# Row maxima of an attention kernel: one negated row at partition 0 by a Prelu, in place of two rows by a Relu

## The chip, the cores and the metric

The kernel runs on one core of a Trainium2 chip. Its metric is the device time of one execution in microseconds (us), and lower is better. Four compute engines work side by side, each in its own program order: PE (TensorE, matmuls), DVE (VectorE), ACT (ScalarE) and POOL (GpSimd). SP issues all DMAs. PEld is PE's loading of the stationary operand, which the profile keeps apart from the matmuls themselves.

## The reference

Attention over pooled queries, then a channel-mixing feed-forward. The sizes are 8 batches, 8 heads, 1152 keys, 576 pooled queries and a head size of 64; the model width is 512 and the hidden width 1024.

```python
q_pool = q.reshape(B, H, S // 2, 2, D).mean(axis=3)
scores = (1 / sqrt(D)) * (q_pool @ k.T)
scores = scores - max(scores, axis=-1, keepdims=True)
attn = exp(scores)
attn = attn / (sum(attn, axis=-1, keepdims=True) + 1e-9)
x = attn @ v                                   # heads side by side: (B, 576, 512)

x_prev = x shifted by one position, zeros in front
xk = mu_k * x + (1 - mu_k) * x_prev            # xr the same with mu_r
kk = maximum(xk @ w_k, 0)
out = sigmoid(xr @ w_r) * (kk * kk @ w_v)
```

## The kernel before, in words

**Precision.** Products are made of fp16 parts. A value is split into a high part and a low part, and the products high x high, high x low and low x high are added in PSUM.

**A block** (`block`, L527) is one head's 96 queries against all its 1152 keys. There are 64 heads of 6 blocks, 384 blocks in all. The keys lie in nine chunks of 128. A block owns one of three PSUM buffers `s`: columns 0 to 127 are scratch, and the nine 128x96 score tiles lie behind them. Its steps, in the order in which they depend on each other:

- L549, PE: nine matmuls, the first half of the scores. The stationary operand is a key chunk `ks1` (high parts of the key in partitions 0 to 63, low parts in 64 to 127), the moving operand is `qT` with the high parts of the queries.
- L556, DVE: the maximum over the nine chunks, `mx` (128x96).
- L559, PE: `mx` as stationary operand against the identity gives the transposed maxima in the scratch columns, 96 partitions by 128.
- L563, DVE: the maximum along the 128 columns, `mb` (96x1): each query's own maximum.
- L579, PE: `mb`, spread over 128 columns, against a scaled negative identity turns the maxima back into a row, which then stands in every partition of the scratch.
- L583, ACT: this row goes into the operand of the second half of the scores, `qlo` (the part of `qT` with the low parts of the queries in partitions 0 to 63). A Relu with a scale per partition (the tile `sign`, +1 and -1) writes two rows, 96 and 97: one holds what is positive and one what is negative of it.
- L592, PE: nine matmuls, the second half: `ks2` against `qlo`. `ks2` has the high key parts in partitions 0 to 63 (a DMA at L505 copies them from `ks1`) and two constant rows at 96 and 97 (`lift`, L405 and L411), which take the maximum off every score within the same matmul.
- L598, ACT: the exponential of the nine tiles into `pf`. L606, POOL: its low part `pl`.

**Around it.** `queries` (L420) and `prep` (L481) load and split a head's inputs. After the first heads a DMA transposes them (L460, L503). `window` (L642) multiplies probabilities with values (L656, L658, L663 on PE), divides (L679 to L682 on DVE), and after each second head turns the result by PE transposes (L692) and copies it out of the PSUM bank `a` into `xt` with four copies (L702, ACT): two of 64x64, two of 128x256. `halves` (L627) does the same for the two ends of a head that do not fill a tile. `ff` makes the feed-forward of a finished batch (all matmuls at L842) while the next batch's attention runs; the last batch's feed-forward runs alone at the end. `weights` decodes the weights early in the program (DMAs at L720; L732, L734 and L749 on ACT, L744 and L747 on DVE).

**What sets the order.** Every piece of work is recorded with `op(engine, cost, function, reads, writes, key)`. The class `Issue` then plays a list schedule with these costs, improves it forwards and backwards, and shifts the priorities of random groups of operations by the numbers in `MOVES`. Each engine issues its instructions in the order that comes out. So the cost that is written beside an operation takes part in the order, and `MOVES`, `BASE`, `SEED`, `SPREAD` and `HALF` choose it.

Of the kernel before, what the change touches and what calls it, by code (L numbers as in the profile page):

```python
# [37 lines left out]
EPS = 2.0 ** -9  # L38
ROW, ROW_N = "AA", 0
# [16 lines left out]
HALF = 1.1  # L56
# [11 lines left out]
SEED, SPREAD = 2, 5.0  # L68
# [227 lines left out]
def kernel(  # L296
# [37 lines left out]
    def bufs(name, n, shape, dt):  # L334
        return [const.tile(shape, dt, name=f"{name}{i}") for i in range(n)]
# [34 lines left out]
    mx, mb, mt = bufs("mx", 3, [P, QN], F16), bufs("mb", 3, [P, 1], F16), bufs("mt", 3, [P, 1], F32)  # L370
# [31 lines left out]
    nc.gpsimd.memset(qn[0][:, 1, :, D:P], 0.0)  # L402
    sign, lift = const.tile([P, 1], F32, name="sign"), const.tile([P, 1], F32, name="lift")
    for c_, a_, b_ in ((sign, -2.0, 1.0), (lift, -2.0 * SM, SM * (1.0 - EPS))):
        nc.vector.tensor_scalar(c_, ident[:, QN + 1:QN + 2], a_, b_, op0=ALU.mult, op1=ALU.add)  # L405
    negd = const.tile([P, P], F16, name="negd")
    nc.gpsimd.tensor_scalar(negd, ident, EPS - 1.0, 1.0, op0=ALU.mult, op1=ALU.mult)
    for t_ in ks2:
        nc.vector.memset(t_[D:P], 0.0)
        nc.vector.memset(t_[QN:QN + 2], 1.0)  # L410
        nc.vector.tensor_scalar(t_[QN:QN + 2], t_[QN:QN + 2], lift[QN:QN + 2], None, op0=ALU.mult)  # L411
# [8 lines left out]
    def queries(n, key):  # L420
# [16 lines left out]
        for j0, j1 in JS:  # L437
            js, jk = slice(j0, j1), range(j0, j1)
            for nj, ck, o_, src in pieces(j0, j1):
# [10 lines left out]
                qn[0][:, 1, js, 0:D], qs[0][:, js], SQ, qn[0][:, 0, js, 0:D], op0=ALU.mult, op1=ALU.subtract),  # L450
# [30 lines left out]
    def prep(n, key):  # L481
# [23 lines left out]
        op("DMA", 0.54, lambda: nc.sync.dma_start(ks2[i][0:D], ks1[i][0:D]),  # L505
# [21 lines left out]
    def block(n, j, i, t):  # L527
# [10 lines left out]
        mxz, mbz, mtz = mx[z], mb[z], mt[z]  # L538
        row = ROW[int(n >= ROW_N)]
# [12 lines left out]
        for c0, c1 in BK:  # L552
# [3 lines left out]
        op("DVE", 0.975, lambda: nc.vector.tensor_reduce(mxz, grid(0, NC).rearrange("p c q -> p q c"),  # L556
                                                         axis=AX.X, op=ALU.max),
           r=[("s", z)], w=[("mx", z)], key=t)
        op("PE", 0.059, lambda: nc.tensor.matmul(s[0:QN, 0:P], mxz, identb, start=False, stop=False,  # L559
                                                 skip_group_check=True),  # L560
           r=[("mx", z)], w=[("s", z)], key=t + O_MAX)
        if row == "A":
            op("DVE", 0.199, lambda: nc.vector.tensor_reduce(mbz[0:QN], s[0:QN, 0:P], axis=AX.X, op=ALU.max),  # L563
               r=[("s", z)], w=[("mb", z)], key=t + O_MAX)
        else:
            op("DVE", 0.199, lambda: nc.vector.tensor_reduce(mtz[0:QN], s[0:QN, 0:P], axis=AX.X, op=ALU.max),
               r=[("s", z)], w=[("mt", z)], key=t + O_MAX)
            op("DVE", 0.07, lambda: nc.vector.tensor_scalar(
                mbz[0:QN], mtz[0:QN], 1.0 + 2.0 * EPS, mtz[0:QN], op0=ALU.mult, op1=ALU.max),
               r=[("mt", z)], w=[("mb", z)], key=t + O_MAX)  # L570
        if row == "D":
            def lower(c0, c1):
                for c in range(c0, c1):
                    nc.tensor.matmul(cols(c, c + 1), mbz[0:QN].broadcast_to([QN, P]), negd[0:QN, 0:QN],
                                     start=False, stop=False, skip_group_check=True)

            op("PE", NC * 0.0430, lambda: lower(0, NC), r=[("mb", z)], w=[("s", z)], key=t + O_MAX)
        else:
            op("PE", 0.047, lambda: nc.tensor.matmul(s[:, 0:QN], mbz[0:QN].broadcast_to([QN, P]),  # L579
                                                     negi[0:QN, 0:QN], start=False, stop=False, skip_group_check=True),  # L580
               r=[("mb", z)], w=[("s", z)], key=t + O_MAX)
            if row == "A":
                op("ACT", 0.267, lambda: nc.scalar.activation(qlo[QN:QN + 2], s[QN:QN + 2, 0:QN], AF.Relu,  # L583
                                                              scale=sign[QN:QN + 2]),
                   r=[("s", z)] + kl, w=qm, key=t + O_MAX)
            else:
                op("ACT", 0.175, lambda: nc.scalar.copy(qlo[QN:QN + 1], s[QN:QN + 1, 0:QN]),
                   r=[("s", z)] + kl, w=qm, key=t + O_MAX)
# [6 lines left out]
        for c0, c1 in BK:  # L595
            op("PE", (c1 - c0) * 0.0430, lambda c0=c0, c1=c1: scores2(c0, c1),
               r=[("ks2", hp)] + kl + (qm if row != "D" else []), w=[("s", z)], key=t + O_EXP)
# [390 lines left out]
```

## Time and profile before

| | |
|---|---|
| Median of 3 runs | 1172.43 us (1170.05 to 1173.1) |
| Profiled execution | 1174.95 us, of which the span from the first to the last instruction is 1173.2 us |
| Busy in the span | PE 1116.6, ACT 947.3, DVE 900.7, POOL 527.5 us |
| TensorE clock granted | 0.987 of full speed over the span, 0.89 between 15 and 150 us |

A row such as `L583 ACT ACTIVATE qT<-s,sign 2x96 f16<-2x96 f32 x384 | 124.7, 332 | 71.5 <-PE s L579 56.9` reads: the line, the engine, the operation, what it writes and reads with shapes, how often; then its busy time in us, the mean duration of one in ns, and the idle time of its engine just before it with what ended most of that. Matmuls overlap: a row's mean is the time from a matmul's start to its result, far more than the distance between two starts. So PE's idle time in these rows is only what is longer than that overlap. The chain of waits is followed back from the last instruction, at each step to what released it.

### The profile page before, as it was taken

Reading aid. Unit: us, or ns where it says so; the run is one execution under the profiler, and the core shown is the slowest. Engines: PE = TensorE matmul, PEld = TensorE weight load, DVE = VectorE, ACT = ScalarE, POOL = GpSimd, SP = SyncE. Lnnn points to the kernel's source line nnn. Section 1 sums busy time; section 2 is a strip of 40 time slices with the busy share of each in tenths; the row PEclk is TensorE's granted clock in tenths of the full one; section 3 lists DMA queues with packets and bytes.
Section 4 is the critical chain, followed back from the end, with each engine's and each line's share of the span. In section 5 each row is a group of like instructions: output and inputs, shape, how many; then the busy total and the mean of one; then the engine's idle time right before and its main releaser. Section 6 shows DMA issues by size and latency. Waiting matters only on the chain.

```text
span 1173.2 us, 44732 instructions
## 1 busy us (share of the span) xinstructions
PE 1116.6 (95%) x18956; PEld 912.8 (78%) x18956; DVE 900.7 (77%) x1849; ACT 947.3 (81%) x1947; POOL 527.5 (45%) x574
## 2 busy tenths in 40 slices
PE   5887799999999999999999999999999999999998
PEld 4776787978788787878787888868797878888665
DVE  8888888888788888887888788777888788774531
ACT  7899988978888888888978887877878788876753
POOL 2456554644445444544443554435354444443111
PEclk9888899999999999999999999999999999999999
DMA  9986756555455643755354435344453734310000
GB/s 204 204 177 159 184 116 126 118 108 131 99 132 112 113 117 81 133 110 136 83 125 94 120 91 129 94 95 103 112 119 70 140 84 92 60 38 10 21 19 27
DMA packets 218744, 125.71 MB, mean 107 GB/s; under 512 B 154032, under 2 KB 190896, under 8 KB 218544
## 3 DMA queue, kind: packets, MB, share of 16 engines
q1 hardware_dynamic: 218544, 122.86, 47.7%
q8 instruction: 148, 2.42, 0.9%
q14 instruction: 52, 0.43, 0.1%
HBM read 67.11 MB, written 9.44 MB: 65 GB/s over the span
## 4 chain that ended last, share of the span: by engine, by line
PE 73%; ACT 12%; DMA 6%; DVE 5%; issue 4%; SPq 0%; ACTq 0%; DVEq 0%
PE f L842 27%; PE s L549 11%; PE s L592 10%; PE a L658 5%; PE a L656 5%; PE a L663 5%; ACT pf L598 4%; PE s L842 4%; DMA ks<-kn 4%; DVE mx L556 2%; ACT qT L583 2%; PE a L627 2%; PE s L559 2%; PE a L842 2%; PE s L579 1%
## 5 line engine op out<-in xcount | busy, mean ns | idle before, releaser
L606 POOL TENSOR_SCALAR pl<-pf 128x864 f16<-128x864 uint16 x384 | 370.4, 965 | 452.3 <-ACT pf L598 419.6
L556 DVE TENSOR_REDUCE mx<-s 128x96 f16<-128x864 f32 x384 | 398.9, 1053 | 97.3 <-PE s L549 59.8
L598 ACT ACTIVATE pf<-s 128x864 int32<-128x864 f32 x384 | 334.9, 889 | 45.3 <-PE s L592 29.4
L549 PE MATMUL s<-qT,ks 128*128 128x96 f16 x3456 | 222.4, 208 | 22.6 <-ACT pf L598 18.0
L549 PEld LDWEIGHTS <-ks 128*128 128x128 f16 x3456 | 188.8, 99 | 58.0 <-issue 32.2
L592 PE MATMUL s<-qT,ks 128*128 128x96 f16 x3456 | 214.4, 208 | 12.4 <-ACT qT L583 10.7
L592 PEld LDWEIGHTS <-ks 128*128 128x128 f16 x3456 | 182.4, 99 | 38.7 <-issue 19.0
L656 PE MATMUL a<-vt,pf 128*128 128x65 f16 x2304 | 196.0, 194 | 1.0 <-DVE a L640 0.6
L658 PE MATMUL a<-vt,pf 128*128 128x64 f16 x2304 | 196.3, 195 | 0.0
L583 ACT ACTIVATE qT<-s,sign 2x96 f16<-2x96 f32 x384 | 124.7, 332 | 71.5 <-PE s L579 56.9
L656 PEld LDWEIGHTS <-pf 128*128 128x128 f16 x2304 | 164.9, 99 | 5.2 <-ACT pf L598 0.5
L658 PEld LDWEIGHTS <-pf 128*128 128x128 f16 x2304 | 157.4, 98 | 7.6 <-issue 1.5
L563 DVE TENSOR_REDUCE mb<-s 96x1 f16<-96x128 f32 x384 | 107.5, 283 | 46.5 <-PE s L559 41.5
L842 PE MATMUL f<-xhk,wk_hi 128*128 128x256 f16 x496 | 135.1, 272 | 1.1 <-ACT r L869 0.7
L842 PE MATMUL f<-xlk,wk_hi 128*128 128x256 f16 x496 | 135.1, 272 | 0.0
L842 PE MATMUL f<-xhk,wk_lo 128*128 128x256 f16 x496 | 135.1, 272 | 0.0
L873 POOL TENSOR_TENSOR gl<-g 128x512 f16<-128x512 f32 x72 | 78.6, 1093 | 107.3 <-ACT g L871 104.4
L663 PE MATMUL a<-vb,pl 128*128 128x65 f16 x2304 | 122.8, 194 | 0.1
L842 PEld LDWEIGHTS <-wk_hi 128*128 128x128 f16 x1152 | 107.0, 98 | 12.9 <-issue 1.3
L663 PEld LDWEIGHTS <-pl 128*128 128x128 f16 x2304 | 97.6, 98 | 4.4 <-POOL pl L606 0.3
L559 PE MATMUL s<-identb,mx 128*96 128x128 f16 x384 | 87.1, 228 | 5.6 <-DVE mx L556 5.3
L842 PE MATMUL f<-wv_hi,g 128*128 128x512 f16 x240 | 90.9, 379 | 0.7 <-ACT em L892 0.6
(113 smaller groups left out, 2046.4 us busy)
## 6 DMA issues: line engine op xcount, KB each, us to landing
kr<-in_k_dram SPq DMA_DIRECT2D x64, 288.0 KB
vr<-in_v_dram SPq DMA_DIRECT2D x64, 288.0 KB
qr<-in_q_dram SPq DMA_DIRECT2D x63, 256.0 KB
ks<-ks SPq DMA_DIRECT2D x64, 144.0 KB
out_dram<-em SPq DMA_DIRECT2D x36, 256.0 KB
st<-in_moe_w_k_dram SPq DMA_DIRECT2D x8, 512.0 KB
st<-in_moe_w_v_dram SPq DMA_DIRECT2D x8, 512.0 KB
qr<-in_q_dram SPq DMA_DIRECT2D x32, 64.0 KB
```

What stands on the lines that cost most here:

```text
L549: nc.tensor.matmul(cols(c, c + 1), ks1[hp][:, c, :], qhi, start=(c == c0), stop=False, skip_group_check=True)
L556: op("DVE", 0.975, lambda: nc.vector.tensor_reduce(mxz, grid(0, NC).rearrange("p c q -> p q c"), axis=AX.X, op=ALU.max), r=[("s", z)], w=[ ...
L559: op("PE", 0.059, lambda: nc.tensor.matmul(s[0:QN, 0:P], mxz, identb, start=False, stop=False, skip_group_check=True), r=[("mx", z)], w=[( ...
L563: op("DVE", 0.199, lambda: nc.vector.tensor_reduce(mbz[0:QN], s[0:QN, 0:P], axis=AX.X, op=ALU.max), r=[("s", z)], w=[("mb", z)], key=t + O ...
L583: op("ACT", 0.267, lambda: nc.scalar.activation(qlo[QN:QN + 2], s[QN:QN + 2, 0:QN], AF.Relu, scale=sign[QN:QN + 2]), r=[("s", z)] + kl, w= ...
L592: nc.tensor.matmul(cols(c, c + 1), ks2[hp][:, c, :], qlo, start=False, stop=True, skip_group_check=True)
L598: op("ACT", NC * QN / 1200 + 0.06, lambda: nc.scalar.activation(pf[:, :, rows], grid(0, NC), AF.Exp, bias=SHIFT, scale=0.125 / (2.0 * SQ)) ...
L606: op(pe, d, lambda: en.tensor_scalar(pl[:, :, rows], half(pf, U16, 0)[:, :, rows], LO, 1.0, op0=ALU.mult, op1=ALU.mult), r=[("pf", x) for ...
L656: nc.tensor.matmul(bank[:, a0:a0 + VN], half(pf, F16, 1)[:, c, rows], vt[jv][:, c, D:D + VN], start=(w == 1 and c == 0 and hh == 0), stop= ...
L658: nc.tensor.matmul(bank[:, a0:a0 + D], half(pf, F16, 1)[:, c, rows], vt[jv][:, c, 0:D], start=False, stop=False, skip_group_check=True)
L663: nc.tensor.matmul(bank[:, a0:a0 + VN], pl[:, c, rows], vb[jv][:, c, 0:VN], start=False, stop=(c == NC - 1), skip_group_check=True)
L842: nc.tensor.matmul(ps, terms[i][0], terms[i][1], start=(first and i == 0), stop=(i == last), skip_group_check=True)
```

## The change

1. **One row by a Prelu.** L583's Relu with the scale tile `sign` becomes a Prelu with two constants, a scale and an `alpha` for negative inputs. It writes one row, of 1x96, at partition 0. The constant row of `ks2` (L407 after) stands at partition 0 too and is written by a single memset. The tiles `sign`, `lift`, `negd` and `mt`, and the variants of the row that did not run, go.
2. **Low query parts in partitions 64 to 127.** `qlo` and the high key parts in `ks2` move from partitions 0 to 63 up to 64 to 127; the DMA that fills `ks2` now goes from partitions 0 to 63 to partitions 64 to 127.
3. **Transposed maxima with 32 zero columns in front.** `mx` becomes 128x128, with its first 32 columns zeroed once. The stationary operand of the transposing matmul has 128 columns where it had 96, its output 128 partitions, `mb` is 128x1, and the matmul that turns it back works over 128 partitions.
4. **Copies.** Of the four copies out of bank `a` after the transposes, the 64x64 one of partitions 64 to 127 moves from ACT to DVE.
5. **Order.** The costs of the row (0.267 to 0.153) and of `halves` (1.1 to 1.02) change, and the numbers that choose the order are new. `EPS`, by which the row's two slopes differ from 1, is 2**-10 where it was 2**-9.

```diff
-EPS = 2.0 ** -9
-ROW, ROW_N = "AA", 0
+EPS = 2.0 ** -10
+ROW = "Prelu"
...
-HALF = 1.1
+HALF = 1.02
...
-    12, 57, 71, 78, 82, 116, 127, 165, 204, 389, 459, 497, 555, 573, 765, 911, 920, 1257, 1370, 1565, 1944,
...
-), 3000000, 1150.0
-SEED, SPREAD = 2, 5.0
+    35, 45, 48, 64, 96, 102, 107, 118, 189, 197, 445, 511, 603, 622, 676, 682, 702, 806, 807, 882, 1095, 1109,
...
+), 4000000, 1150.0
+SEED, SPREAD = 2, 3.0
...
-    mx, mb, mt = bufs("mx", 3, [P, QN], F16), bufs("mb", 3, [P, 1], F16), bufs("mt", 3, [P, 1], F32)
+    mx, mb = bufs("mx", 3, [P, P], F16), bufs("mb", 3, [P, 1], F16)
...
-    nc.gpsimd.memset(qn[0][:, 1, :, D:P], 0.0)
-    sign, lift = const.tile([P, 1], F32, name="sign"), const.tile([P, 1], F32, name="lift")
-    for c_, a_, b_ in ((sign, -2.0, 1.0), (lift, -2.0 * SM, SM * (1.0 - EPS))):
-        nc.vector.tensor_scalar(c_, ident[:, QN + 1:QN + 2], a_, b_, op0=ALU.mult, op1=ALU.add)
-    negd = const.tile([P, P], F16, name="negd")
-    nc.gpsimd.tensor_scalar(negd, ident, EPS - 1.0, 1.0, op0=ALU.mult, op1=ALU.mult)
+    nc.gpsimd.memset(qn[0][:, 1, :, 0:D], 0.0)
+    for t_ in mx:
+        nc.vector.memset(t_[:, 0:P - QN], 0.0)
     for t_ in ks2:
-        nc.vector.memset(t_[D:P], 0.0)
-        nc.vector.memset(t_[QN:QN + 2], 1.0)
-        nc.vector.tensor_scalar(t_[QN:QN + 2], t_[QN:QN + 2], lift[QN:QN + 2], None, op0=ALU.mult)
+        nc.vector.memset(t_[0:D], 0.0)
+        nc.vector.memset(t_[0:1], SM)
...
-        op("DMA", 0.54, lambda: nc.sync.dma_start(ks2[i][0:D], ks1[i][0:D]),
+        op("DMA", 0.54, lambda: nc.sync.dma_start(ks2[i][D:P], ks1[i][0:D]),
...
-        op("DVE", 0.975, lambda: nc.vector.tensor_reduce(mxz, grid(0, NC).rearrange("p c q -> p q c"),
+        op("DVE", 0.975, lambda: nc.vector.tensor_reduce(mxz[:, P - QN:P], grid(0, NC).rearrange("p c q -> p q c"),
                                                          axis=AX.X, op=ALU.max),
...
-        op("PE", 0.059, lambda: nc.tensor.matmul(s[0:QN, 0:P], mxz, identb, start=False, stop=False,
-                                                 skip_group_check=True),
+        op("PE", 0.059, lambda: nc.tensor.matmul(s[:, 0:P], mxz, identb, start=False, stop=False, skip_group_check=True),
...
+        op("DVE", 0.199, lambda: nc.vector.tensor_reduce(mbz, s[:, 0:P], axis=AX.X, op=ALU.max),
+           r=[("s", z)], w=[("mb", z)], key=t + O_MAX)
+        op("PE", 0.047, lambda: nc.tensor.matmul(s[:, 0:QN], mbz.broadcast_to([P, P]), negi[:, P - QN:P],
+                                                 start=False, stop=False, skip_group_check=True),
+           r=[("mb", z)], w=[("s", z)], key=t + O_MAX)
+        op("ACT", 0.153, lambda: nc.scalar.activation(qlo[0:1], s[0:1, 0:QN], getattr(AF, ROW),
+                                                      scale=1.0 - EPS, alpha=(1.0 + EPS) / (1.0 - EPS)),
+           r=[("s", z)] + kl, w=qm, key=t + O_MAX)
...
-                op("ACT", 0.051 + (q1 - q0) / 1200, lambda ps=ps, q0=q0, q1=q1, f0=f0, x_=x_: nc.scalar.copy(
+                up = y == 1
+                op("DVE" if up else "ACT", 0.07 + HW / 960 if up else 0.051 + (q1 - q0) / 1200, lambda up=up, ps=ps, q0=q0, q1=q1, f0=f0, x_=x_: (nc.vector.tensor_copy if up else nc.scalar.copy)(
                     x_[ps, 1 + q0:1 + q1], bank[ps, f0:f0 + q1 - q0]),
                    r=[ka], w=[("xt", b % 3, g, y)], key=t + O_TURN)
```

How the order moves is shown at three places. In the rows a number behind a name tells buffers apart.

The first is DVE at the start of the program, from the first head's low key parts to the first maximum. Before:

```order
L496 TENSOR_TENSOR kn_76<-kr_70,kn_76 128x4x64
L513 SCALAR_TENSOR_TENSOR vt_85<-vr_72,vt_85 128x4x64
L442 TENSOR_TENSOR qs_75<-qr_74 128x128
L405 TENSOR_SCALAR sign<-ident 128x1
L405 TENSOR_SCALAR lift<-ident 128x1
L411 TENSOR_SCALAR ks_0_81<-ks_0_81,lift 2x1152
L411 TENSOR_SCALAR ks_1_82<-ks_1_82,lift 2x1152
L478 COPY ks_0_79<-s_138 128x512
```

After the change, the same place:

```order
L492 TENSOR_TENSOR kn_76<-kr_70,kn_76 128x5x64
L438 TENSOR_TENSOR qs_75<-qr_74 128x128
L438 TENSOR_TENSOR qs_75<-qr_74 128x192
L445 SCALAR_TENSOR_TENSOR qn_78<-qs_75,qn_78 128x2x64
L404 MEMSET mx_93 128x16
L474 COPY ks_0_79<-s_135 128x512
```

The four instructions on `sign`, `lift` and `ks2` between the first key parts and the copy of the transposed keys are gone. The value split `vt` moves behind; the second query sum, the first low query parts and one memset of `mx` move ahead of the copy.

The second is ACT in the stage in which the weights are decoded, around the first copies into `xt`. Before:

```order
L517 ACTIVATE vb_89<-vr_72 128x9x64
L583 ACTIVATE qT_84<-s_136,sign 2x96
L702 COPY xt_106<-a 128x256
L702 COPY xt_106<-a 64x64 x2
L810 ACTIVATE tmp_123<-xt_106,omu_k 128x256
L598 ACTIVATE pf<-s_136 128x9x96
L732 ACTIVATE f<-st_129 128x512
L583 ACTIVATE qT_84<-s_138,sign 2x96
```

After the change:

```order
L678 COPY xt_103<-a 128x256
L678 COPY xt_103<-a 64x64
L561 ACTIVATE qT_84<-s_133 1x96
L708 ACTIVATE f<-st_126 128x512
L678 COPY xt_103<-a 128x256
L710 ACTIVATE em_124<-st_126 128x512
L573 ACTIVATE pf<-s_133 128x9x96
L513 ACTIVATE vb_89<-vr_72 128x9x64
L786 ACTIVATE tmp_120<-xt_103,omu_k 128x256
```

The two 64x64 copies of a turn have become one on ACT, and the row (L583, after it L561) reads no scale tile. The copies and the decoding have moved ahead of the splitting of the values `vb`.

The third is DVE at the same turn, where the copy that left ACT now stands (L678). Before:

```order
L679 TENSOR_SCALAR den_103<-a 128x5
L556 TENSOR_REDUCE mx_93<-s_136 128x96
L681 RECIPROCAL den_103<-den_103 128x5
L682 TENSOR_TENSOR xb_104<-a,den_103 128x5x64
L563 TENSOR_REDUCE mb_96<-s_136 96x1
L513 SCALAR_TENSOR_TENSOR vt_85<-vr_73,vt_85 128x5x64
L556 TENSOR_REDUCE mx_95<-s_138 128x96
```

After the change:

```order
L657 TENSOR_TENSOR xb_101<-a,den_100 128x5x64
L551 TENSOR_REDUCE mx_93<-s_133 128x96
L445 SCALAR_TENSOR_TENSOR qn_78<-qs_75,qn_78 128x4x64
L556 TENSOR_REDUCE mb_96<-s_133 128x1
L678 COPY xt_103<-a 64x64
L551 TENSOR_REDUCE mx_94<-s_134 128x96
L551 TENSOR_REDUCE mx_95<-s_135 128x96
```

The copy stands between the maximum of one block and the two long maxima of the next two blocks, which wait behind it in DVE's queue.

More of the change, by code (lines that the diff above doesn't have):

```diff
@@ L449, in queries @@
             op("DVE", (j1 - j0) * D / 960 + 0.069, lambda js=js: nc.vector.scalar_tensor_tensor(
-                qn[0][:, 1, js, 0:D], qs[0][:, js], SQ, qn[0][:, 0, js, 0:D], op0=ALU.mult, op1=ALU.subtract),
+                qn[0][:, 1, js, D:P], qs[0][:, js], SQ, qn[0][:, 0, js, 0:D], op0=ALU.mult, op1=ALU.subtract),
                r=[("qs", c) for c in jk] + [("qn", c) for c in jk], w=[("qnl", c) for c in jk], key=key + 2, port=True)
@@ L537, in block @@
         rows, us = slice(p0, p0 + QN), range(p0 // U, (p0 + QN) // U)
-        mxz, mbz, mtz = mx[z], mb[z], mt[z]
-        row = ROW[int(n >= ROW_N)]
+        mxz, mbz = mx[z], mb[z]
         def cols(c0, c1):
@@ L561, in block @@
            r=[("mx", z)], w=[("s", z)], key=t + O_MAX)
[L562 to L588, printed above, removed]
+        op("DVE", 0.199, lambda: nc.vector.tensor_reduce(mbz, s[:, 0:P], axis=AX.X, op=ALU.max),
+           r=[("s", z)], w=[("mb", z)], key=t + O_MAX)
@@ L596, in block @@
             op("PE", (c1 - c0) * 0.0430, lambda c0=c0, c1=c1: scores2(c0, c1),
-               r=[("ks2", hp)] + kl + (qm if row != "D" else []), w=[("s", z)], key=t + O_EXP)
+               r=[("ks2", hp)] + kl + qm, w=[("s", z)], key=t + O_EXP)
         op("ACT", NC * QN / 1200 + 0.06, lambda: nc.scalar.activation(
```

10 rows, old and new, of the table AHEAD2 are left out of this document.

## The prediction, made before the changed kernel ran

> **What bounds the kernel now.** I read the busy table first.
>
> ```profile
> span 1173.2 us, 44732 instructions
> PE 1116.6 (95%) x18956; PEld 912.8 (78%) x18956; DVE 900.7 (77%) x1849; ACT 947.3 (81%) x1947; POOL 527.5 (45%) x574
> ```
>
> PE is idle for 1173.2 - 1116.6 = 56.6 us, so anything that only takes work off ACT or DVE must pay through these 56.6 us or through idle time too short to show behind the overlap of matmuls. The view by stages tells where they lie (columns: time, then busy us and instructions of each engine, granted clock, DMA share):
>
> ```profile
> core 0: us, PE busy (x) PEld busy (x) DVE busy (x) ACT busy (x) POOL busy (x), PEclk, DMA share, GB/s
> 0.00:15.00 15.00, 6.44 (x68) 5.28 (x69) 12.21 (x37) 9.92 (x22) 2.11 (x10) 1.00 0.74 209
> 15.00:150.00 135.00, 106.37 (x2121) 95.21 (x2121) 115.50 (x232) 125.24 (x242) 74.28 (x77) 0.89 0.83 181
> 150.00:1075.00 925.00, 909.39 (x16119) 754.20 (x16117) 740.78 (x1518) 763.87 (x1581) 437.25 (x474) 1.00 0.48 104
> 1075.00:1173.20 98.20, 94.45 (x652) 58.06 (x650) 32.22 (x64) 48.28 (x104) 13.86 (x14) 1.00 0.06 22
> ```
>
> PE's idle time is 8.6 us in the start, 28.6 in the stage with the weight decoding (15 to 150 us), 15.6 in the long middle and 3.7 in the last feed-forward, where no block runs. In the second stage ACT is the fullest engine, 125.2 of 135 us, and in its core it hardly pauses:
>
> ```profile
> 60.00:90.00 30.00, 24.73 (x504) 21.78 (x501) 26.26 (x50) 29.19 (x55) 17.42 (x19) 0.89 0.93 177
> 90.00:120.00 30.00, 23.03 (x456) 20.62 (x453) 24.09 (x48) 29.31 (x58) 19.30 (x20) 0.89 0.64 167
> ```
>
> 58.5 of 60 us: that stage is ACT's. In the middle PE itself is the bound. PE's longest waits (who waited for whom, us in total, times, longest), between 15 and 150 us:
>
> ```profile
> PE s L549 <- ACT pf L598: 12.6, 24, 1.1
> PE s L592 <- ACT qT L583: 6.7, 15, 0.9
> ```
>
> and between 150 and 1075 us:
>
> ```profile
> PE s L549 <- ACT pf L598: 5.4, 12, 1.4
> PE s L592 <- ACT qT L583: 4.0, 6, 1.4
> ```
>
> The chain of waits by line, for the start and the two attention stages:
>
> ```profile
> by line: DVE ks L410 13.6%; issue 12.8%; PE s L549 10.7%; DVE ks L409 7.2%; ACT vt L510 7.0%; DVE ks L411 6.4%; ACT qT L475 5.1%; ACT ks L475 4.8%; ACT vb L517 3.8%; ACT qn L445 3.5%; DVE kn L496 3.2%; ACT kn L493 3.1%; DVE ks L478 2.9%; AC
> ...
> by line: ACT pf L598 13.7%; issue 11.4%; PE s L549 10.4%; DVE mx L556 7.7%; PE s L592 6.5%; ACT qT L583 5.4%; ACT f L732 5.0%; ACT em L734 4.9%; PE a L656 3.8%; PE a L658 3.6%; DMA ks<-ks 3.6%; PE a L663 2.8%; ACT vt L510 2.5%; DMA ks<-kn 2
> ...
> by line: PE f L842 32.2%; PE s L549 12.1%; PE s L592 11.3%; PE a L663 5.3%; PE a L658 5.2%; PE a L656 5.2%; DMA ks<-kn 4.8%; ACT pf L598 3.5%; issue 2.8%; PE a L627 2.2%; PE s L559 1.8%; DVE mx L556 1.6%; ACT qT L583 1.6%; PE s L579 1.3%; P
> ```
>
> So L583, the instruction that changes, is on the chain for 5.4% of 135 = 7.3 us in the second stage and 1.6% of 925 = 14.8 us in the middle.
>
> **The change part by part.** The groups that carry the prices:
>
> ```profile
> L583 ACT ACTIVATE qT<-s,sign 2x96 f16<-2x96 f32 x384 | 124.7, 332 | 71.5 <-PE s L579 56.9 <-DVE mb L563 2.9 <-DVE xm L813 2.0
> L702 ACT COPY xt<-a 128x256 f32<-128x256 f32 x64 | 23.7, 370 | 1.3 <-PE a L692 0.5
> L702 ACT COPY xt<-a 64x64 f32<-64x64 f32 x64 | 13.2, 206 | 7.6 <-PE a L692 6.8
> L640 DVE TENSOR_TENSOR a<-a,xlb 128x64 f32<-128x64 f32 x32 | 7.2, 226 | 10.4 <-ACT xlb L639 10.4
> L559 PEld LDWEIGHTS <-mx 128*96 128x96 f16 x384 | 47.7, 125 | 16.8 <-DVE mx L556 8.8
> L549 PEld LDWEIGHTS <-ks 128*128 128x128 f16 x3456 | 188.8, 99 | 58.0 <-issue 32.2 <-ACT ks L475 1.7 <-DMA ks<-kn 0.6
> L579 PEld LDWEIGHTS <-mb 96*128 96x128 f16 x384 | 37.6, 99 | 13.5 <-DVE mb L563 5.2
> L413 DVE MEMSET vt<- 128x18 f16 x3 | 0.1, 73 | 0.1
> L493 ACT ACT_TABLE_LOAD x1 | 1.3, 1283 | 0.7 <-PEq L972 0.7
> ```
>
> *The row.* The trace has no Prelu. The nearest rows are L702's copies, which also read PSUM on ACT and take no tile as scale: 206 ns for 64 columns and 370 for 256, so 164/192 = 0.85 ns a column, and 206 + 32 x 0.85 = 233 ns for 96. Another function and type may add a little; I take 237, and 95 ns less than 332. The bounds are 206 (126 less) and 332 (nothing). How many there are in each stage, from the stage view of L583 alone:
>
> ```profile
> 15.00:150.00 135.00, 16.76 (x52) 0.89 0.83 181
> 150.00:1075.00 925.00, 107.61 (x331) 1.00 0.48 104
> ```
>
> Second stage: 52 x 0.095 = 4.9 us off ACT, and 4 of the 64x64 copies with 0.8 us. If the chain stays as it is, its share of L583 shrinks by 95/332, 7.3 x 0.29 = 2.1 us; if ACT bounds every microsecond, 5.7. ACT is at 93%, so I take 4. Middle: 331 x 0.095 = 31.4 us off ACT, but ACT has 161 us of idle time there, and most of this only lengthens its own waits. By the chain it is 14.8 x 0.29 = 4.2 us; the ceiling is what PE visibly waits behind ACT there, 5.4 + 4.0 = 9.4; the floor is 0. I take 4.
>
> *The start.* The pieces of the chain that the change touches:
>
> ```profile
> 6.31 0.95 DVE ks L411 x2
> 7.29 0.43 DVE ks L478
> ```
>
> L411's two instructions (0.95 us) go, and so does what makes their operand; the order shown with the change has the copy of the transposed keys directly behind the query sums. The memset of the constant row stays, with one partition instead of two over as many columns, so I leave its price as it is. Behind L411 ACT's own copy of the keys waits, and then the first block. I take 1 us; the bounds are 0 (the value and query work of ACT ends last anyway) and 1.5.
>
> *Loading the maxima.* 125 ns for 96 columns, 99 for 128 in every other load of that kind. What of these 26 ns reaches the matmuls shows in order of time:
>
> ```profile
> 604.94 0.27 PE L842 MATMUL f<-xhk,wk_lo 128*128 128x256 f16 x1
> ...
> 605.05 0.27 PE L842 MATMUL f<-xhk,wk_hi 128*128 128x256 f16 x1
> ...
> 605.77 0.23 PE L559 MATMUL s<-identb,mx 128*96 128x128 f16 x1
> ...
> 605.84 0.28 PE L663 MATMUL a<-vb,pl 128*128 128x65 f16 x4
> ```
>
> 256 columns take 0.11 us from start to start, so 128 take 0.055; here L559 holds the next matmul off for 0.07. That is 0.015 x 384 = 5.8 us if it holds for all of them, nothing where the neighbours are long enough to cover the load. I take 2.5. L579's load now spans 128 partitions where it had 96, and L563 reduces 128: the columns stay as they are, and L549 loads 128 partitions in the same 99 ns in which L579 loads 96. I count both as nothing.
>
> *The moved copy.* L702's second 64x64 copy leaves ACT 32 times and comes to DVE 32 times. DVE on the same bank takes 226 ns for 64 columns (L640): 7.2 us more for an engine that is 86% busy in the second stage and 80% in the middle. DVE waits for the transposes in front of it, and behind it in the queue stand the long maxima of the next two blocks, for which PE waits in turn. Cover is DVE's idle time, 20 us in the second stage and 184 in the middle; I charge 0.5 us, with bounds of -1 (bank `a` is free 0.2 us sooner, since the two copies now run side by side) and 14, worked out below.
>
> *Zero columns, the shifted partitions, the DMA.* The three memsets take 3 x 0.073 = 0.2 us (L413's size) at a time when DVE waits for the first keys, 0.2 if it does not. The DMA that fills `ks2` moves the same bytes; were the shifted one slower, the 3.6% of the chain that it holds in the second stage, 4.9 us, would grow. I count both as nothing. *The new order* has no price of its own in this trace. It can lose what it wins; I count it as 0 and widen the range by 6 each way, a tenth of PE's idle time.
>
> **The sum:** -4 - 4 - 1 - 2.5 + 0.5 = -11 us against the profiled 1174.95 us (span 1173.2 and 1.75 around it), that is 1164. This execution lies 2.5 us above the median of the runs, so in their terms 1172.43 - 11 = 1161.5 us.
>
> **The rivals.**
>
> *More than I count (1144 us).* The second stage packs anew: at the 97% that ACT reaches in its core, (125.2 - 5.7)/0.975 = 122.6 us in place of 135, 12.4 less; all 9.4 us of waits behind ACT in the middle go; the start gives 1.5 and the loads 5.8. That makes 29, 1143.5. For it speaks that the stage's clock is 0.89 and would rise with a denser PE; against it that DVE, at 115.5 us, is close behind ACT, and that the DMA engines are busy 83% there. On the clock, this trace has 0.89 in that stage while the waits of PE quoted above are 1.1 us at the longest. The Trainium skill (TensorE: Matmul & The Clock Gate, Part 1: The HAM clock gate) has the clock halved only after an idle window of about 3.4 us. By that rule no wait quoted there would cost clock and nothing would come back with the shorter row, so that this rival would lose that argument; the trace's 0.89 does not agree with the rule as it stands.
>
> *The saving falls into ACT's idle time (1170 us).* ACT waits for L579 before L583:
>
> ```profile
> ACT qT L583 <- PE s L579: 56.9, 65, 3.6
> ```
>
> If these waits just grow, only the start and a part of the loads remain, 1 to 3 us. For it speaks that PE is 98% busy in the middle; against it that the second stage is plainly ACT's.
>
> *The Prelu is no cheaper than the Relu was (1171 us).* If `alpha` costs what the scale tile cost, 332 ns stay, while the order was laid out for a row that takes 0.114 us less; then the loads and the start are all there is, less what the too early matmuls wait.
>
> *DVE holds the maxima up (1182 us).* The place is the moved copy. Each of the 32 puts its own 0.226 us and the wait for the transposes (6.8 us, all that ACT waited before its 64x64 copies) into a queue with a long maximum behind it: 7.2 + 6.8 = 14 us. With the row's gain in the middle gone at the same time, since a late maximum makes the whole chain of the block late, it is +14 - 2 (second stage) - 1 - 1 = +10, 1182. It decides the sign from the point at which more than 11 of the 14 us reach PE. Against it speaks DVE's idle time around it.
>
> *A table switch (2160 us).* If Prelu and Exp could not stand in ACT's tables together, each block would load twice: 384 x 2 x 1.283 = 985 us. The program before has one load (L493, 1283 ns), and so has the order after the change. The Trainium skill (ScalarE: Activation LUTs, Table sets: the hidden batching unit) says that functions are loaded in named sets and that each change of set costs a load; it does not say in which set Prelu is. By its rule it is the loads in the program that count, and there is one.
>
> **How the numbers follow.** My forecast 0.59, more than counted 0.10, ACT's idle time 0.15, a dear Prelu 0.05, DVE 0.10, the tables 0.01. About 0.3% (3.5 us) is what a measurement of this kernel can tell from no change. Faster by more than that, under 1168.9: 0.59 + 0.10 and a fifth of the third case, 0.72. Slower, over 1175.9: DVE and the tables, 0.11. The rest, 0.17, is within. The likeliest case alone spans 1153 to 1170 (half its sum, 5.5 us, for its terms and 6 for the order, added as squares: 8 us). To hold 8 in 10 the range goes up past the cases with no gain and down most of the way to the larger one: 1147 to 1176.
>
> **What would show it.** The Prelu's row: 230 to 250 ns, one partition. The load of `mx`: 99 ns. ACT some 40 us less busy over the span (36.5 for the row, 6.6 for the copies, less a little), DVE some 6 more. The second stage's work done by about 146 us, told by how late the last weight is decoded; PE's waits for the row near 5 us in place of 10.7. The forecast is wrong if PE's idle time stays at 56 us although the row is short: then the gain went into ACT's waits. It is wrong to the other side if waits of L559's successor for the maximum grow, or if PE waits for DVE around the moved copy.

## The result, and the profile after

The changed kernel takes 1145.04 us (median of 4 runs, 1142.71 to 1147.61) against 1172.55 us for the kernel before beside it: ratio 0.977, 95% interval 0.9745 to 0.9795. That is 27.5 us less, where 11 were forecast. The profiled execution took 1144.73 us. Its span and busy table:

```profile
span 1142.9 us, 44742 instructions
PE 1094.8 (96%) x18956; PEld 896.5 (78%) x18956; DVE 933.3 (82%) x1880; ACT 846.4 (74%) x1915; POOL 515.8 (45%) x573
```

Three readings. ACT is 947.3 - 846.4 = 100.9 us less busy, where "some 40" were expected. PE's idle time fell only from 56.6 to 48.1 us, 8.5 of the 30.3 us by which the span is shorter; the other 21.8 us left PE's *busy* time, with the same 18956 matmuls. And DVE is 32.6 us busier, where 6 were expected.

The view by stages, with the last cut put behind the last block as before:

```profile
core 0: us, PE busy (x) PEld busy (x) DVE busy (x) ACT busy (x) POOL busy (x), PEclk, DMA share, GB/s
0.00:15.00 15.00, 5.80 (x58) 4.92 (x58) 9.62 (x31) 8.14 (x18) 1.80 (x9) 1.00 0.67 189
15.00:150.00 135.00, 109.60 (x2278) 96.38 (x2278) 130.30 (x252) 118.12 (x257) 78.54 (x83) 0.95 0.75 186
150.00:1047.00 897.00, 887.21 (x16032) 739.17 (x16030) 760.48 (x1535) 674.08 (x1541) 422.80 (x469) 1.00 0.48 107
1047.00:1142.90 95.90, 92.14 (x599) 56.07 (x595) 32.88 (x64) 46.05 (x101) 12.66 (x13) 1.00 0.06 23
```

The middle gave most. Before, PE was busy there for 909.39 us over 16119 matmuls, 56.42 ns each; now 887.21 us over 16032, 55.34 ns each: 1.08 ns x 16032 = 17.3 us out of PE's busy time. Its idle time went from 15.6 to 9.8 us, another 5.8. Together 23 us. The second stage now holds 157 more matmuls in its 135 us, at a granted clock of 0.95 in place of 0.89. They take 48.1 ns of PE's busy time each in place of 50.2 (109.60 us over 2278, 106.37 over 2121), some 4.6 us in all, and how much of this is the clock is not separated. The stage's fullest engine is now DVE, with 130.3 us.

The groups that the prediction priced (durations in ns behind the comma):

```profile
L561 ACT ACTIVATE qT<-s 1x96 f16<-1x96 f32 x384 | 87.3, 231 | 82.2 <-PE s L558 79.2 <-DVE vt L509 1.7
L554 PEld LDWEIGHTS <-mx 128*128 128x128 f16 x384 | 37.3, 98 | 24.7 <-DVE mx L551 16.2
L678 DVE COPY xt<-a 64x64 f32<-64x64 f32 x32 | 7.3, 229 | 4.0 <-ACT xt L678 1.6 <-PE a L667 1.1 <-PE s L558 0.5
```

The row takes 231 ns, the load of `mx` 98, the copy on DVE 229: each price was right. So the time came from something that none of them holds. Each ACT timeline below has a start and a duration in us for every instruction. Of the kernel before:

```profile
127.58 0.89 ACT L598 ACTIVATE pf<-s 128x864 int32<-128x864 f32 x1 [0.73 <-POOL pl L606]
128.50 0.33 ACT L583 ACTIVATE qT<-s,sign 2x96 f16<-2x96 f32 x1
128.85 0.70 ACT L734 ACTIVATE em<-st 128x512 int32<-128x512 uint32 x1
```

and of the changed kernel:

```profile
100.42 0.90 ACT L573 ACTIVATE pf<-s 128x864 int32<-128x864 f32 x1
101.19 0.22 ACT L561 ACTIVATE qT<-s 1x96 f16<-1x96 f32 x1
101.32 0.76 ACT L506 ACTIVATE vt<-vr 128x320 f16<-128x320 f32 x2
```

Before, the row started 0.03 us after its predecessor's end (127.58 + 0.89 = 128.47), and its successor 0.02 us after its own end. Now it starts 0.13 us *before* its predecessor ends, and its successor starts 0.09 us before it ends. From the start and end of all 384 rows: before, the median gap was 25 ns on each side; now the median is an overlap of 93 ns ahead and 92 behind. Where nothing has to be waited for, a row thus took 25 + 333 + 25 = 383 ns between its neighbours and now takes 234 - 93 - 92 = 49. The prediction saw 95 of these 334 ns. Not every row gains as much: 255 of the 384 overlap the one ahead and 231 the one behind, and over all of them the median time between the neighbours went from 383 to 142 ns.

### The profile page after: what moved, and what is told of

It reads as the page before. It is cut to its first block, busy times and chain, and to the rows that moved or that the text cites. A ratio compares the mean times of both kernels' runs of the same rounds, so it can differ in the third digit from the quotient of the medians.

```text
span 1142.9 us, 44742 instructions
## 1 busy us (share of the span) xinstructions
PE 1094.8 (96%) x18956; PEld 896.5 (78%) x18956; DVE 933.3 (82%) x1880; ACT 846.4 (74%) x1915; POOL 515.8 (45%) x573
## 4 chain that ended last, share of the span: by engine, by line
PE 78%; DMA 5%; DVE 2%; ACT 2%; issue 1%; SPq 0%; POOL 0%; ACTq 0%; DVEq 0%
PE f L818 32%; PE s L567 10%; PE s L544 10%; PE a L638 5%; PE a L633 5%; PE a L631 5%; PE s L818 4%; DMA ks<-kn 3%; PE a L602 2%; PE a L818 2%; PE s L554 1%; PE a L667 1%; DMA qT<-qn 1%; PE s L558 1%; DVE mx L551 1%
## 5 line engine op out<-in xcount | busy, mean ns | idle before, releaser
L581 POOL TENSOR_SCALAR pl<-pf 128x864 f16<-128x864 uint16 x384 | 366.3, 954 | 445.0 <-ACT pf L573 413.4
L551 DVE TENSOR_REDUCE mx<-s 128x96 f16<-128x864 f32 x384 | 400.2, 1053 | 76.6 <-PE s L544 48.1
L544 PEld LDWEIGHTS <-ks 128*128 128x128 f16 x3456 | 183.6, 98 | 37.6 <-issue 12.8
L567 PEld LDWEIGHTS <-ks 128*128 128x128 f16 x3456 | 180.3, 99 | 29.1 <-issue 10.2
L561 ACT ACTIVATE qT<-s 1x96 f16<-1x96 f32 x384 | 87.3, 231 | 82.2 <-PE s L558 79.2
L556 DVE TENSOR_REDUCE mb<-s 128x1 f16<-128x128 f32 x384 | 108.6, 287 | 25.0 <-PE s L554 21.6
L849 POOL TENSOR_TENSOR gl<-g 128x512 f16<-128x512 f32 x72 | 75.8, 1054 | 98.4 <-ACT g L847 95.3
L554 PE MATMUL s<-identb,mx 128*128 128x128 f16 x384 | 83.5, 221 | 9.3 <-DVE mx L551 8.5
L818 PE MATMUL f<-wv_hi,gl 128*128 128x512 f16 x240 | 91.0, 379 | 0.0
```

The costliest lines, as they stand in the source:

```text
L544: nc.tensor.matmul(cols(c, c + 1), ks1[hp][:, c, :], qhi, start=(c == c0), stop=False, skip_group_check=True)
L551: op("DVE", 0.975, lambda: nc.vector.tensor_reduce(mxz[:, P - QN:P], grid(0, NC).rearrange("p c q -> p q c"), axis=AX.X, op=ALU.max), r=[( ...
L554: op("PE", 0.059, lambda: nc.tensor.matmul(s[:, 0:P], mxz, identb, start=False, stop=False, skip_group_check=True), r=[("mx", z)], w=[("s" ...
L556: op("DVE", 0.199, lambda: nc.vector.tensor_reduce(mbz, s[:, 0:P], axis=AX.X, op=ALU.max), r=[("s", z)], w=[("mb", z)], key=t + O_MAX)
L561: op("ACT", 0.153, lambda: nc.scalar.activation(qlo[0:1], s[0:1, 0:QN], getattr(AF, ROW), scale=1.0 - EPS, alpha=(1.0 + EPS) / (1.0 - EPS) ...
L567: nc.tensor.matmul(cols(c, c + 1), ks2[hp][:, c, :], qlo, start=False, stop=True, skip_group_check=True)
```

## The experiments

What makes the row stand alone? It was read at first as the scale tile's doing, which the Prelu does without; against it stood the place of the row (partition 96 before, 0 now), the new order, and the load of the maxima. The kernels undo or do one of these each; a ratio is to the kernel before in runs beside it.

**Prelu alone, at partition 96, in the order before.**

```diff
-activation(qlo[QN:QN + 2], s[QN:QN + 2, 0:QN], AF.Relu, scale=sign[QN:QN + 2])
+activation(qlo[QN:QN + 1], s[QN:QN + 1, 0:QN], AF.Prelu, scale=1.0 - EPS, alpha=(1.0 + EPS) / (1.0 - EPS))
...
```

> The kernel before with the Prelu's single row alone (scale and alpha as constants, still at partition 96; one constant row in ks2); every instruction stands in the order of before. Theory A (the Relu with the scale tile ran alone on ACT: 25 ns of nothing on either side of it, where other neighbours overlap by some 93 ns; so the row took about 380 ns out of ACT and now takes about 140): ACT's busy time falls by 85 to 100 us, ends of neighbours overlap with the row, time 1148 to 1156. Theory B (the row saves its 95 ns and no more; the rest of the gain is the new order): ACT's busy time falls by some 37 us, time 1163 to 1168. Theory C (all of it is the new order): 1170 to 1175.

Measured: 1158.15 us, ratio 0.9846 (0.9823 to 0.9869). The row, in the view by groups:

```profile
L582 ACT ACTIVATE qT<-s 1x96 f16<-1x96 f32 x384 | 90.9, 242 | 76.4 <-PE s L578 62.2 <-DVE mb L562 2.8 <-DVE xm L812 2.0
```

It is 90 ns shorter and still stands alone, with median gaps of 24 and 25 ns. So no scale tile, and no overlap. Yet this alone is worth 18 us (0.0154 x 1172.55): the shorter row, with the two scaled constant rows that fall away, gives more than twice the 8 us that the prediction had for the row. ACT is 947.3 - 906.7 = 40.6 us less busy, near the 37 of theory B, but the time lies below that theory's range.

**The Relu with its scale tile, in the changed kernel**, two rows at partitions 0 and 1.

```diff
-activation(qlo[0:1], s[0:1, 0:QN], getattr(AF, ROW), scale=1.0 - EPS, alpha=...)
+activation(qlo[0:2], s[0:2, 0:QN], AF.Relu, scale=sign[0:2])
...
```

> The changed kernel with the Relu and its scale tile put back (two rows, at partitions 0 and 1, with two constant rows in ks2); every other instruction stands in the order of the changed kernel. Theory A: the row is alone on ACT again, ACT's busy time rises by some 90 us, time 1163 to 1172. Theory B: 1150 to 1155. Theory C: 1145 to 1148. If the isolation is a matter of partition 96 and not of the scale tile, the row overlaps here although it has the tile, and the time is 1150 to 1155 with ACT some 37 us busier.

Measured: 1150.15 us, 0.9781 (0.975 to 0.9813), which can't be told from the changed kernel.

```profile
L565 ACT ACTIVATE qT<-s,sign 2x96 f16<-2x96 f32 x384 | 121.9, 324 | 75.8 <-PE s L562 72.2 <-DVE vt L513 2.2
```

324 ns, with the scale tile, and it overlaps both neighbours, by 93 and 92 ns at the median. The scale tile costs duration, but it does not isolate. That theory fell.

**Wider maxima alone**: `mx` of 128 columns in the order before.

```diff
-bufs("mx", 3, [P, QN], F16)
+bufs("mx", 3, [P, P], F16)
...
```

> The kernel before with the maxima padded to 128 columns alone (zero columns behind, the transposing matmul writes 128 partitions); the order is that of before. The load of the maxima takes 99 ns in place of 125. If the prediction's term holds, 2.5 us less (0 to 5.8): 1167 to 1172.

Measured: 1175.62 us, 0.9997 (0.9984 to 1.0011). The load is as short as in the changed kernel, and nothing comes of it:

```profile
L561 PEld LDWEIGHTS <-mx 128*128 128x128 f16 x384 | 37.7, 98 | 16.5 <-DVE mx L558 8.3
```

**Six forms of the row in one kernel**, a sixth of the blocks each: Relu with tile (L585) or constant (L587), Prelu (L589), Copy with tile (L591), Relu at partition 64 (L593), a plain copy (L595).

> The kernel before in its own order, with six forms of the row's instruction in turn over the blocks (the maximum is not taken off rightly in most blocks, so the output is not the reference's): a Relu with the scale tile on two rows at partition 96, a Relu with a constant scale there, a Prelu with constants on one row there, a Copy with the scale tile on two rows there, a Relu with the scale tile on two rows at partition 64, and a plain copy of one row at 96. If the scale tile isolates an instruction, the first, fourth and fifth have 25 ns of nothing before and after, and the others overlap by about 93 ns. If partition 96 does, only the fifth overlaps. If two rows do, the third and sixth overlap. If the function with the tile does (Relu), the first and fifth are isolated and the Copy is not.

Measured, in one run: 1168.14 us. The groups of the six:

```profile
L591 ACT ACTIVATE qT<-s,sign 2x96 f16<-2x96 f32 x64 | 21.4, 334 | 12.7 <-PE s L579 8.2 <-DVE mb L563 2.8
L585 ACT ACTIVATE qT<-s,sign 2x96 f16<-2x96 f32 x64 | 21.3, 333 | 10.9 <-PE s L579 9.4
L593 ACT ACTIVATE qT<-s,sign 2x96 f16<-2x96 f32 x64 | 21.3, 332 | 14.4 <-PE s L579 10.7 <-DVE xm L826 2.0
L587 ACT ACTIVATE qT<-s 2x96 f16<-2x96 f32 x64 | 15.5, 243 | 18.1 <-PE s L579 16.6 <-DVE ex L910 0.5
L589 ACT ACTIVATE qT<-s 1x96 f16<-1x96 f32 x64 | 15.5, 242 | 13.9 <-PE s L579 11.6 <-DVE vt L513 1.0 <-DVE xlr L834 0.2
L595 ACT CAST qT<-s 1x96 f16<-1x96 f32 x64 | 14.8, 232 | 5.0 <-PE s L579 3.6
```

The tile adds 90 ns whatever the function (333 against 243), one or two rows are alike, and a plain copy is 10 ns shorter. All six, at partition 64 (L593) or 96, have a median gap of 24 or 25 ns ahead and behind. Function, tile and number of rows are out; what they share is that none starts at partition 0. That gave the theory which the next runs test.

The same trace narrows it. Where one row stands directly behind another and both begin at partition 96, they overlap; here the Prelu starts 0.09 us before the Relu ahead of it ends (721.24 + 0.24 = 721.48):

```profile
721.24 0.24 ACT L587 ACTIVATE qT<-s 2x96 f16<-2x96 f32 x1 [0.89 <-PE s L579]
721.39 0.23 ACT L589 ACTIVATE qT<-s 1x96 f16<-1x96 f32 x1
```

The same holds in the kernel before: of its 55 rows that directly follow another row, 30 overlap it, by up to 92 ns, and of the 329 that follow anything else none does. A row at 96 stands alone because nearly all its neighbours begin at partition 0.

**The places alone, then the Prelu too, in the order before.** The first keeps the Relu and its tile but moves the rows to partitions 0 and 1, with the low query parts at 64 to 127 and the zero columns in front; the second makes the row a Prelu.

```diff
-activation(qlo[QN:QN + 2], s[QN:QN + 2, 0:QN], AF.Relu, scale=sign[QN:QN + 2])
+activation(qlo[0:2], s[0:2, 0:QN], AF.Relu, scale=sign[0:2])
...
```

> The kernel before in its own order with only the places moved: low query parts in partitions 64 to 127, maxima behind 32 zero columns, and the Relu with its scale tile on two rows at partitions 0 and 1. Theory D (an ACT instruction that does not begin at partition 0 overlaps with neither neighbour; at partition 0 it does): the row keeps some 327 ns but overlaps by 93 ns on both sides, ACT's busy time falls by 60 to 75 us, time 1155 to 1162. Theory A (it is the scale tile): the row stays alone and the time is that of before, 1172 to 1177.

> As the run with the places moved, and the Prelu in place of the Relu; still the order of before. Theory D: ACT's busy time falls by another 25 to 35 us, to about 860; the time is 3 to 6 us below the run with the places moved, 1150 to 1158. If the gain were additive with that of the Prelu alone at partition 96 (16.8 us), it would be about 1143.

Measured: places alone 1152.93 us, 0.9784 (0.9752 to 0.9817); with the Prelu 1147.39 us, 0.9757 (0.9735 to 0.9779). In both the row overlaps its neighbours by 92 or 93 ns at the median. ACT's busy time falls by 62.1 and another 27.3 us, as theory D forecast, and both times lie below its ranges. The places alone, which leave the row's duration nearly as it was (327 in place of 333 ns), give 25 us; the Prelu on top of them gives 3, within the intervals. No new order and no copy on DVE is needed for the whole gain.

**The copy on DVE as well, in the order before.**

```diff
-lambda ps=ps, ...: nc.scalar.copy(
+lambda y=y, ps=ps, ...: (nc.vector.tensor_copy if y == 1 else nc.scalar.copy)(
```

> As the run before it, and the 64x64 copy of partitions 64 to 127 is made by DVE in the slot that ACT's copy had in the order of before. It too did not begin at partition 0 and stood alone on ACT. Theory D: ACT falls by another 8 to 12 us; the time changes by -2 to +1 us. The rival of the prediction (DVE holds the maxima up): 3 to 10 us slower. What is left between this run and the changed kernel is the new order.

Measured: 1159.07 us, 0.9856 (0.9828 to 0.9884): 11.6 us slower than without it (0.0099 x 1172.55). In the view of waits (who waited for whom, us in total, times, longest) ACT now has

```profile
ACT xt L703 <- DVE xt L703: 14.6, 21, 1.4
```

where the kernel without the moved copy has no such wait. The two 64x64 copies do not run side by side; the one on ACT waits for the one on DVE, and ACT's queue with it. That these waits make up the 11.6 us is not shown.

**The changed kernel again**, beside the last three.

> The changed kernel once more, on the chip of these runs, so that the last step (the new order and nothing else) can be read beside the others: 1143 to 1148. If the order has no part in the gain, it equals the run with the copy on DVE; by theory D with an order worth half of the rest, it is 4 to 10 us faster than that.

Measured: 1149.86 us, 0.9776 (0.9749 to 0.9804), not told apart from the old order with the places and the Prelu (0.9757). The new order with the copy on DVE wins nothing beyond these.

**Reading and writing apart**: three Prelus in turn, which read and write partitions 0 and 0 (L587), 0 and 32 (L589), 32 and 0 (L591).

> The kernel with the places moved and the Prelu, in the order of before, with three forms in turn over the blocks (in a third of the blocks the maximum is not taken off, so the output is not the reference's): a Prelu that reads and writes partition 0; one that reads partition 0 and writes partition 32; one that reads partition 32 and writes partition 0. If what is written must begin at partition 0 for an overlap, the second alone stands apart with gaps of 25 ns; if what is read must, the third alone; if both, the second and the third. If 32 is not like 64 and 96, all three overlap by 93 ns.

Measured, in one run: 1152.82 us. Three places of ACT's timeline:

```profile
96.61 0.88 ACT L607 ACTIVATE pf<-s 128x864 int32<-128x864 f32 x1
97.51 0.24 ACT L591 ACTIVATE qT<-s 1x96 f16<-1x96 f32 x1
97.66 0.67 ACT L743 ACTIVATE em<-st 128x512 int32<-128x512 uint32 x1
...
101.40 0.67 ACT L519 ACTIVATE vb<-vr 128x576 f16<-128x576 f32 x1
102.09 0.24 ACT L589 ACTIVATE qT<-s 1x96 f16<-1x96 f32 x1
102.35 0.62 ACT L758 CAST wr_hi<-ex 128x512 f16<-128x512 f32 x1
...
112.71 0.73 ACT L447 ACTIVATE qn<-qs 128x640 f16<-128x640 f32 x1
113.33 0.22 ACT L587 ACTIVATE qT<-s 1x96 f16<-1x96 f32 x1
113.46 0.86 ACT L607 ACTIVATE pf<-s 128x864 int32<-128x864 f32 x1
```

L587 starts before 113.44, its predecessor's end, and its successor starts before 113.55, its own. L589 never overlaps, on either side, in 128 cases. L591 never starts before the one ahead ends, while the next starts before its end in a third of the cases, as here (97.66 against 97.75). Writing at 32 isolates on both sides; reading there isolates for certain from the one ahead. Behind L591 it is decided by what the next one reads. Of 56 successors that read SBUF, as `em<-st` does here, 42 overlap it, and the other 14 start over 100 ns after its end; of 72 that read PSUM, as L591 does, none overlaps.

This run also parts the row's partition from the other places, which all stay as in the kernel with places and Prelu. It is 0.982 of the kernel before beside it (1173.96 us), 0.0063 x 1172.55 = 7.4 us slower than 0.9757. Two thirds of the rows are isolated here, on one side at least, and two thirds of the 10.4 us between the Prelu at 96 and at 0 (0.9846 - 0.9757) are 7. As far as a single run tells, it is the row's partition that carries the gain, and not the low query parts or the DMA that moved with it.

**The changed kernel with the places of before**: its order, its Prelu and its copies, the row at partition 96.

```diff
-activation(qlo[0:1], s[0:1, 0:QN], getattr(AF, ROW),
+activation(qlo[QN:QN + 1], s[QN:QN + 1, 0:QN], getattr(AF, ROW),
...
```

> The changed kernel, its order and its Prelu and its copy on DVE, with the places as they were before (low parts in partitions 0 to 63, maxima in 96 columns, the row at partition 96). Theory D: the row stands alone on ACT again, ACT's busy time rises by some 45 us, and as in the order of before the place is worth 8 to 13 us: 1156 to 1162. If the new order makes up for it, 1148 to 1152.

Measured: 1169.52 us, 0.9956 (0.9939 to 0.9973), above the range that theory D gave. Its busy table:

```profile
PE 1111.2 (95%) x18956; PEld 910.8 (78%) x18956; DVE 915.7 (78%) x1877; ACT 898.2 (77%) x1915; POOL 521.5 (45%) x573
```

ACT is 51.8 us busier than in the changed kernel with its places, and PE waits for it more often. PE's two longest waits for ACT (us in total, times, longest) are

```profile
PE s L542 <- ACT pf L571: 14.1, 33, 1.3
PE s L565 <- ACT qT L559: 11.4, 19, 1.5
```

where the changed kernel has 7.8 and 7.5 us.

The row stands alone again, with median gaps of 24 and 25 ns, and the changed kernel loses 0.0186 x 1172.55 = 21.8 us of its 27.5. Most of the gain needs the places, the row's at partition 0 among them. The new order is worse than the old for a row at 96 (0.9956 against 0.9846, though the copy on DVE differs too).

**The copy back on ACT, in the changed kernel**, in the slot where it stands.

```diff
-lambda up=up, ...: (nc.vector.tensor_copy if up else nc.scalar.copy)(
+lambda up=up, ...: nc.scalar.copy(
```

> The changed kernel with the 64x64 copy of partitions 64 to 127 back on ACT, in the slot that it has on DVE; all other rows in the same order. In the order of before the copy on DVE cost 11 us. If that is the copy's own doing, this run is 5 to 11 us faster than the changed kernel (1138 to 1145); if it was the old order, which had no room for the copy on DVE, this run is -2 to +4 us beside it (1147 to 1154).

Measured: 1151.19 us, 0.9809 (0.9788 to 0.983). The interval overlaps that of the changed kernel (0.9745 to 0.9795): in its own order the copy on DVE costs nothing, and may gain a little. Order and copy hang together: with the copy on ACT the new order is 6.1 us slower than the old (0.9809 against 0.9757), with the copy on DVE 10.1 us faster (0.977 against 0.9856).

**The old second copy started at partition 0**: the kernel with places and Prelu in the old order, its 64x64 copy of partitions 64 to 127 made one of all 128. Where the two copies stand in the other order, it overwrites the lower half of `xt`, so those values aren't the reference's.

```diff
-ps = slice(y * HW, (y + 1) * HW) if y < 2 else slice(0, P)
+ps = slice(0, (P, HW)[y]) if y < 2 else slice(0, P)
...
```

> The run with the places moved and the Prelu in the order of before, and the copy that began at partition 64 made of all 128 partitions (its lower half is overwritten by the copy behind it, which begins at partition 0 as before), so that no copy of ACT begins anywhere but at partition 0. Theory D: ACT's busy time falls by some 3 to 6 us; the time by 0 to 2 us, to 1145 to 1148, at or below both kernels. If the place of the copy does not matter, ACT's busy time rises by 0 to 1 us.

Measured: 1146.91 us, 0.977 (0.9749 to 0.9791), no different from 0.9757. ACT's busy time falls from 857.9 to 854.1 us, 3.8 / 32 = 119 ns a copy, but 32 copies are too few to show in the time.

The time by place and form of the row, as ratios:

| | order before, copies on ACT | changed order, one copy on DVE |
|---|---|---|
| Relu with tile, partition 96 | 1 | not run |
| Prelu, partition 96 | 0.9846 | 0.9956 |
| Relu with tile, partition 0 | 0.9784 | 0.9781 |
| Prelu, partition 0 | 0.9757 | 0.977, again 0.9776 |

## Why the prediction was right in its direction and wrong in its size

- **The step that failed: "Zero columns, the shifted partitions, the DMA": "I count both as nothing."** It weighs the memsets and the DMA, and has no term for what the shift does to the row on ACT. The shift puts the row at partition 0, where its neighbours begin, and there it overlaps them. The places alone are worth 25 us in the old order, and in the changed kernel taking them away loses 21.8. The prediction had the row's duration and the stages' busy times, but read no gap between neighbours: three rows of the timeline of before (0.89 ending at 128.47, the row at 128.50) show the isolation, which a row's mean can't.
- **The middle's ceiling, 9.4 us, failed too.** It was the sum of PE's visible waits for ACT. The prediction's first part itself allowed for "idle time too short to show", and the ceiling left it out. The gain in the middle was 23 us, 17.3 of it from PE's busy time. The Prelu alone, at 96, shows the same: its span is 17.2 us shorter (1156.0), and PE's busy time 11.3 (1105.3).
- **The row's 95 ns was right in duration** (332 to 231, 101). It was mis-sized in worth: -8 predicted, 18 measured alone, but 3 where the place has been moved already. The two don't add; both take work off ACT, and why the second brings so little is not shown.
- **The second stage** was about right: its rows -4 and the start -1 are 5 us, and the 60th exponential comes 7.1 us earlier (161.5 against 168.6). By the 384th it is 30.7 us. The weights' last decoding, forecast "by about 146", comes at 138.3. In the views of single lines the columns are durations in ns (shortest, median, longest), then the first and last start in us; before:

```profile
L749 ACT CAST wv_hi<-ex x8: 614/619/626, 111.9 to 152.9; 128x512 f16<-128x512 f32 x8
```

  and after:

```profile
L725 ACT CAST wv_hi<-ex x8: 601/614/618, 102.3 to 138.3; 128x512 f16<-128x512 f32 x8
```

- **The start: -1 predicted.** The first exponential comes 1.7 us later, not earlier, and only from the eleventh block on are all of them earlier; before:

```profile
L598 ACT ACTIVATE pf<-s x384: 863/890/925, 16.2 to 1073.7; 128x864 int32<-128x864 f32 x192
```

  and after:

```profile
L573 ACT ACTIVATE pf<-s x384: 862/890/914, 17.9 to 1043.0; 128x864 int32<-128x864 f32 x192
```

- **The loading of the maxima: -2.5 predicted.** Duration right (125 to 98 ns), worth nothing: the interval of the wider maxima alone ends at 0.9984, 1.9 us. That the neighbours cover the load is likely but not shown.
- **The moved copy: +0.5, with 14 as its upper bound.** In the changed order it costs nothing that can be measured. In the old order it cost 11.6 us, so the rival that had DVE hold things up was real in its price, and the new order takes it away. Its detail was wrong: ACT waits for DVE's copy. "The two copies now run side by side" was wrong as well.
- **The new order, 0 with 6 either way,** holds for order and copy together: with places and Prelu in both, 0.977 and 0.9776 stand against 0.9757 in the old one. Taken apart, the order loses 6.1 us with the copy on ACT and wins 10.1 with it on DVE.
- **The rivals.** "More than I count" gave 1143.5 us, within 2 us of the result, but by luck: the second stage was to give 12.4 us and the middle 9.4, and the middle gave 23. The clock of the second stage did rise, as it said. "The saving falls into ACT's idle time" is refuted by the Prelu alone. No table switch came.
- **What would show it.** PE's waits for the row fell from 10.7 to 7.5 us over the span, where 5 were expected. "PE's idle time" was the wrong mark: it fell by 8.5 us only while the time fell by 27.5.

## What to carry to other kernels

Price a small instruction by the time between its neighbours, the end of the one ahead to the start of the one behind, not by its duration: here up to 334 ns a row fell away between the neighbours, and 101 of them were duration. On ACT, let small instructions in a busy queue begin at the partition at which those around them begin (here 0), and lay out the operands around that. Where a bound engine shows little idle time, its visible waits are no ceiling; compare its busy time per instruction, which held about 70% of the gain here (21.8 of 30.3 us).

## What the runs showed of the hardware that was not expected

Among neighbours that begin at partition 0, a row on ACT that reads and writes at partition 64 or 96, or writes at 32, stands alone (median gaps of 24 to 25 ns), while one that reads and writes at partition 0 overlaps both, by 92 to 94 ns. At 96 and at 0 this was seen for the Relu with its tile on two rows and for the Prelu on one row; at 96 also for Copy and a plain copy. What counts is not partition 0 itself but whether the start changes, in SBUF and PSUM each for itself. In the changed kernel with the row at 96, all else on ACT begins at partition 0, and 795 of ACT's instructions begin, in what they read or write, at another partition than the last one on ACT that read or wrote the same memory: none of them starts before the one ahead has ended. Of the 1118 others 954 do. At partition 96 the row's duration is also some 9 ns longer (243 against 234 at the median). What in the engine does this isn't shown.

The Trainium skill (ScalarE: Activation LUTs, What ACT_TABLE_LOAD costs) says that instructions of this kind overlap by about 93 ns when they stand back to back, and that each operand of one value per partition adds about 93 ns. The traces agree at partition 0 (92 to 94) and on the operand (333 against 243 at partition 96, 324 against 231 at 0); between neighbours that begin at different partitions the measurement differs (24 to 25 ns of nothing), and it decides.

DVE's 32.6 us more are not explained. The copies are 7.3 of them. The long maximum takes 1053 ns in both kernels; the groups that grew most have two tensors as inputs, `vt` of 128x256 for one from 465 to 540 ns. The kernel with only the places moved, in the old order and with no copy on DVE, has 933.6 us of DVE, and the changed order with the row at 96 has 915.7. So most of it goes with the places, but no run here isolates its cause.
